# Half-swapped V by DMA instead of GpSimd, first loads dealt anew over three queues, a warm-up on a constant and new scheduler durations, in a fused attention and gated-MLP kernel

## The chip, the cores and the metric

One core of one Trainium2 chip. The metric is the device time of one launch in microseconds (us); the median of several executions is quoted, with the lowest and the highest.

## The reference, cut to what matters

```python
# x: 1 x 2048 x 512, bf16; 32 heads of 16; 4 segments of 512 rows; F = 1792
q, k, v = x @ wq, x @ wk, x @ wv              # split into heads and segments
for s in range(4):                            # segments, in order
    p = softmax(qs @ ks.T * scale + causal_mask)
    a_dot = p @ vs                            # "PV"
    a_mem = (phi(qs) @ M) / (phi(qs) @ z + 1e-6)
    o = sigmoid(beta) * a_mem + (1 - sigmoid(beta)) * a_dot
    M, z = M + phi(ks).T @ vs, z + phi(ks).sum()   # the memory ("mz")
a = concat(o) @ wo
b = (relu(x @ W_gate) * (x @ W_up)) @ W_down
g = sigmoid((x * gate_w).sum(-1))             # one gate per row
out = g * a + (1 - g) * b
```

The memory carries from segment to segment; everything else is free to be interleaved.

## The kernel before: the parts that matter

The program is a list of operations with dependencies, assumed durations and buffers. A small scheduler orders them at build time, engine by engine. So a changed duration, dependency or buffer count changes the whole order on every engine.

PV contracts over 64 keys at a time in a 64 x 32 tiling. For half of the blocks the V rows stand in the wrong half of the partitions, so a second copy of V with the halves swapped (VS) is kept. Before, GpSimd made it, two copies for each of 16 blocks of 128 rows:

```python
    def proj_v(s, t):                       # V of segment s, rows 128*t..
        ...
        if t == 0:
            VS[s] = Buf(VSp)                # VSp: 2 buffers, only the heads needed
        for r in range(2):
            def f(e, r=r):
                src = Vp[s].t[64 - 64 * r:128 - 64 * r, t, 0:H * HP]...   # the other half
                nc.gpsimd.tensor_copy(VS[s].t[64 * r:64 * r + 64, t, ...], src[:, :, r, 0:DH])
```

The start: x in four parts on the SyncE and ScalarE queues, wq in three parts on GpSimd's, 28 warm-up matmuls on a tile that VectorE first sets, and wk held back by a dependency until a copy of x is done:

```python
    for i in range(2):
        for eng, q, h in (("SP", nc.sync, 0), ("ACT", nc.scalar, 1)):
            ...                              # x part (i, h)
    for n, (c0, c1) in enumerate(((0, 1), (1, 2), (2, 4))):
        ...  nc.gpsimd.dma_start(out=wq_sb[:, c0:c1, :], ...)
    o_wk0 = op("wk0", {"DVE": 0.08}, ..., key=-490)        # opens wk's load

    def c_dummy(e):
        for _ in range(28):
            nc.tensor.matmul(g_dummy.t[:, 0:P], lhsT=zero[:, 0:P], rhs=zero[:, 0:P], ...)
```

Three transfers on SyncE's queue: the transposes of phi(k) (tile pK) that feed the memory update, the load of the next segment's x (tile xn) that feeds the row gate g, and the weights of the MLP.

```python
                nc.sync.dma_start_transpose(out=pK[s].t[:, :, c * P:(c + 1) * P], in_=src.t[:])
    ...
            nc.sync.dma_start(out=xn[s].t[:], in_=x[s * L:(s + 1) * L, :]...)
```

The softmax here doesn't subtract the row's maximum and nothing guards it: scores larger than these inputs give would overflow.

Of the kernel before, what the change touches and what calls it, by code (L numbers as in the profile page):

```python
# [26 lines left out]
VSW = H // 2 * HP + 16  # L27

MM = 0.216
SW = 0.1  # L30
# [136 lines left out]
def kernel(  # L167
# [52 lines left out]
    VSp = pool("VS", 2, [P, 4, VSW])  # L220
# [5 lines left out]
    zero = osp.tiles[0]  # L226
# [25 lines left out]
    def c_zero(e):  # L252
        nc.vector.memset(zero[:, 0:P], 1.0)  # L253
    o_zero = op("zero", {"DVE": 0.15}, c_zero, cls=0, key=-100)
# [7 lines left out]
    def c_warm(e):  # L262
        nc.scalar.activation(scratch[:], zero[:, 0:1], ACT.Exp)
# [10 lines left out]
    def c_vones(e):  # L274
        for t in Vpp.tiles + VSp.tiles:
            nc.gpsimd.memset(t[:].rearrange("p a b -> p (a b)"), 1.0)
    o_vones = op("vones", {"POOL": 6.2}, c_vones, key=-60)
# [11 lines left out]
    def c_dummy(e):  # L289
        for _ in range(28):  # L290
            nc.tensor.matmul(g_dummy.t[:, 0:P], lhsT=zero[:, 0:P], rhs=zero[:, 0:P], start=True, stop=True)  # L291
# [21 lines left out]
    for i in range(2):  # L313
        for eng, q, h in (("SP", nc.sync, 0), ("ACT", nc.scalar, 1)):
            def f(e, i=i, q=q, h=h):
                q.dma_start(out=xn[0].t[:, 2 * h:2 * h + 2, 256 * i:256 * i + 256],
                            in_=x[256 * h:256 * h + 256, 256 * i:256 * i + 256].rearrange("(t p) d -> p t d", p=P))
            lx0[i, h] = load(f"x0_{i}{h}", f, 131072, -300 + i, eng=eng, alloc=[xn[0]] if (i, h) == (0, 0) else [],
                             uses=[] if (i, h) == (0, 0) else [xn[0]])
    for n, (c0, c1) in enumerate(((0, 1), (1, 2), (2, 4))):  # L320
        def f(e, c0=c0, c1=c1):
            nc.gpsimd.dma_start(out=wq_sb[:, c0:c1, :], in_=A_wq[c0 * P:c1 * P, :].rearrange("(c p) n -> p c n", p=P))
        o = op(f"wq{c0}", {"POOL": 1.0}, f, key=-110 + 15 * n, cls=0, land=131072 * (c1 - c0) / GBs)
        for ci in range(c0, c1):
            lwq[ci] = [o]
    o_vones.deps.append((lwq[3][0], -1e9))
# [8 lines left out]
    o_wk0 = op("wk0", {"DVE": 0.08}, lambda e: nc.vector.memset(wk_sb[0:1, 0, 0:1], 0.0), key=-490, cls=0)  # L335
# [67 lines left out]
    for ci in range(NC):  # L403
        def f(e, ci=ci):
            for c in range(NC):
                nc.tensor.matmul(qS.t[:, c, :], lhsT=wq_sb[:, ci, c * P:(c + 1) * P], rhs=xT[0].t[:, ci, :],  # L406
                                 start=(ci == 0), stop=(ci == NC - 1))
        o_q0 = op(f"q0.{ci}", {"PE": 4 * MM * (1.5 if ci < 2 else 1)}, f,
                  deps=xc0[ci] + lwq[ci] + [(o_q0, 0.0) if ci else None],
                  key=-400 + ci, mode="D", alloc=[qS] + q0 if ci == 0 else [], uses=([] if ci == 0 else [qS]) + [xT[0]])  # L410
        if ci < 2:
            first_x(ci + 2, o_q0)
# [165 lines left out]
    def proj_v(s, t):  # L578
# [12 lines left out]
        if t == 0:  # L591
            VS[s] = Buf(VSp)
        o_vs[s, t] = []
        for r in range(2):
            def f(e, r=r):
                src = Vp[s].t[64 - 64 * r:128 - 64 * r, t, 0:H * HP].rearrange("p (h r v) -> p h r v", r=2, v=HP)
                nc.gpsimd.tensor_copy(  # L597
                    VS[s].t[64 * r:64 * r + 64, t, 0:H // 2 * HP].rearrange("p (h v) -> p h v", v=HP)[:, :, 0:DH],
                    src[:, :, r, 0:DH])
            o_vs[s, t].append(op(f"vs{s}{t}{r}", {"POOL": 0.5}, f, deps=[o_v[s, t]] + (o_vs[s, t - 1] if t else []),  # L600
                                 key=a.key + 4, cls=2, alloc=[VS[s]] if t == 0 and r == 0 else [],
                                 uses=[Vp[s]] + ([] if t == 0 and r == 0 else [VS[s]])))
# [13 lines left out]
    def mz_deps(s):  # L616
        return [o_pKt[s, c] for c in range(NC)] + [o_v[s, t] for t in range(4)]
# [21 lines left out]
    def mz0():  # L639
        g = Buf(G)  # L640
        k = dkey(3)
        a = op("mz0", {"PE": 0.5}, lambda e: mz_mm(0, g), deps=mz_deps(0), key=k, mode="C", alloc=[g], uses=[pK[0], Vp[0]])
        mz_after(0, a, g, k)
# [76 lines left out]
    def unit(i):  # L720
# [8 lines left out]
        for n, parts in enumerate(FL):  # L729
# [12 lines left out]
            a = op(f"f{s}{c}.{n}", {"PE": MM}, f,  # L742
# [36 lines left out]
    def dens(s, k0, org):  # L779
# [12 lines left out]
        if mds:  # L792
            gm = Buf(G)
            rec_of[s, "mz"] = am = op(f"mz{s}", {"PE": 0.5}, lambda e: mz_mm(s, gm), deps=[(a, 0.0)], key=k0 - 20, mode="C",
                                      alloc=[gm], uses=[pK[s], Vp[s]])
            gate_mz.append((s, am, gm, k0))
# [34 lines left out]
    def rest(i, E, masks, behind):  # L831
# [4 lines left out]
        def f(e):  # L836
            for kb in range(8):
                src, off = E[kb]
                w = L - 64 * kb
                for r in range(2):  # L840
                    rows = slice(64 * r, 64 * r + 64)
                    for j in range(4):
                        if kb % 2 == r:
                            h = 8 * c + 2 * j + r
                            v = Vp[s].t[rows, kb // 2, h * HP:h * HP + 32]
                        else:
                            h = 4 * c + j
# [3 lines left out]
        a = op(f"pv{s}{c}", {"PE": 1.05}, f,  # L851
               deps=[(m, MG) for m in masks] + [o_v[s, t] for t in range(4)] + [o for t in range(4) for o in o_vs[s, t]] +
# [172 lines left out]
```

## Time and profile before

| | before |
|---|---|
| time, median of six (lowest to highest) | 266.87 us (266.46 to 267.45) |
| span of the profiled execution | 265.3 us |
| TensorE busy | 257.0 us |
| ScalarE, GpSimd, VectorE busy | 193.9, 191.0, 183.8 us |
| warm-up ends and x is transposed | 4.08 us |
| q's first step, k's first matmul | 5.19, 9.60 us |

The prediction below shows the lines of the page, the waits and the start. These are two lines of the timeline of the kernel before, first SyncE's queue, then VectorE. The columns of the timeline are start and duration in us, engine (SPq is SyncE's queue), line, operation, output and input, count, and in brackets the idle time before it and what ended it.

```profile
22.71 0.37 SPq L359 DMA_DIRECT2D xn<-in_A_x_dram  x1
...
28.27 0.75 DVE L461 SCALAR_TENSOR_TENSOR xn<-xn,gwrep 128x512 bf16<-128x512 bf16 x1
```

Segment 1's x is issued at 22.71 and VectorE begins the row gate on it at 28.27, with no bracket: it did not wait. The load landed at 26.16, so it had 2.1 us to spare.

### The profile page before, as it was taken

Reading aid. Unit: us, or ns where it says so; the run is one execution under the profiler, and the core shown is the slowest. Engines: PE = TensorE matmul, PEld = TensorE weight load, DVE = VectorE, ACT = ScalarE, POOL = GpSimd, SP = SyncE. Lnnn points to the kernel's source line nnn. Section 1 sums busy time; section 2 is a strip of 40 time slices with the busy share of each in tenths; the row PEclk is TensorE's granted clock in tenths of the full one; section 3 lists DMA queues with packets and bytes.
Section 4 is the critical chain, followed back from the end, with each engine's and each line's share of the span. In section 5 each row is a group of like instructions: output and inputs, shape, how many; then the busy total and the mean of one; then the engine's idle time right before and its main releaser. Section 6 shows DMA issues by size and latency. Waiting matters only on the chain.

```text
span 265.3 us, 7048 instructions
## 1 busy us (share of the span) xinstructions
PE 257.0 (97%) x2808; PEld 115.9 (44%) x2844; DVE 183.8 (69%) x407; ACT 193.9 (73%) x189; POOL 191.0 (72%) x470
## 2 busy tenths in 40 slices
PE   8999999999999999999999999999999999999995
PEld 6433444444454444444434434344443444344444
DVE  1497888888975285998888837688985735566611
ACT  3598999899885558999896668898788566777010
POOL 8678888888559788798648988887878866537000
PEclk9999999999999999999999999999999999999999
DMA  5997990017310100000551010000000010000011
GB/s 162 289 252 203 313 261 13 4 40 80 100 26 1 42 20 22 0 2 2 132 88 23 21 42 20 4 2 0 2 0 4 0 42 23 20 2 0 2 41 40
DMA packets 27057, 15.54 MB, mean 59 GB/s; under 512 B 13584, under 2 KB 26896, under 8 KB 27024
## 3 DMA queue, kind: packets, MB, share of 16 engines
q1 hardware_dynamic: 26304, 14.30, 22.0%
q0 software_dynamic: 176, 0.52, 0.6%
q8 instruction: 22, 0.36, 0.6%
q10 hardware_dynamic: 544, 0.26, 0.3%
q14 instruction: 11, 0.09, 0.1%
HBM read 9.84 MB, written 2.10 MB: 45 GB/s over the span
## 4 chain that ended last, share of the span: by engine, by line
PE 97%; issue 2%; DVE 0%; ACT 0%; DVEq 0%
PE G L248 74%; PE S L738 9%; PE G L849 7%; PE G L246 3%; PE S L406 2%; PE G L291 1%; PE G L611 1%; PE G L785 0%; PE G L385 0%; DVE os L700 0%; ACT xT L395 0%; DVE os L253 0%; DVE mcole L268 0%; DVEq L700 0%; DVE mcol L267 0%
## 5 line engine op out<-in xcount | busy, mean ns | idle before, releaser
L752 ACT ACTIVATE E<-S 128x2048 bf16<-128x2048 f32 x72 | 135.1, 1876 | 34.3 <-PE S L738 31.9
L760 POOL TENSOR_SCALAR_AFFINE_SELECT E<-E 64x256 bf16<-64x256 bf16 x256 | 115.7, 452 | 38.5 <-ACT E L752 24.6
L248 PE MATMUL G<-xT,wu_sb 128*128 128x512 bf16 x211 | 57.3, 380 | 0.4 <-issue 0.2
L248 PE MATMUL G<-xT,wg_sb 128*128 128x512 bf16 x206 | 56.2, 380 | 1.1 <-issue 0.8
L663 DVE TENSOR_TENSOR hT<-G,os 128x512 bf16<-128x512 f32 x56 | 38.2, 684 | 19.7 <-ACT os L659 10.7
L248 PE MATMUL G<-wd_sb,hT 128*128 128x512 bf16 (+1 forms) x212 | 48.9, 365 | 1.1 <-issue 1.0
L884 DVE STREAM_TRANSPOSE T<-G 128x512 f32<-128x512 f32 x44 | 30.3, 702 | 14.0 <-PE G L849 8.2
L659 ACT ACTIVATE os<-G 128x512 bf16<-128x512 f32 x56 | 32.7, 597 | 6.1 <-PE G L248 5.3
L248 PEld LDWEIGHTS <-wu_sb 128*128 128x128 bf16 x218 | 19.9, 98 | 24.8 <-issue 3.0
L248 PEld LDWEIGHTS <-wg_sb 128*128 128x128 bf16 x218 | 19.4, 98 | 24.6 <-issue 4.1
L248 PEld LDWEIGHTS <-hT 128*128 128x128 bf16 x222 | 20.3, 98 | 22.3 <-issue 2.6
L738 PE MATMUL S<-QT,K 32*128 32x192 bf16 (+7 forms) x512 | 28.6, 287 | 0.5
L738 PEld LDWEIGHTS <-K 32*128 32x128 bf16 x512 | 8.2, 92 | 30.4 <-issue 29.9
L700 DVE TENSOR_SCALAR os<-G,ngcol 128x512 bf16<-128x512 f32 (+1 forms) x10 | 7.0, 697 | 19.4 <-PE G L248 19.3
L849 PE MATMUL G<-E,Vp 64*32 64x128 bf16 (+7 forms) x512 | 19.0, 284 | 0.2 <-issue 0.2
L849 PE MATMUL G<-E,VS 64*32 64x128 bf16 (+7 forms) x512 | 18.4, 284 | 0.0
L248 PE MATMUL G<-wo_sb,oT 128*128 128x512 bf16 (+1 forms) x66 | 17.2, 367 | 0.3 <-issue 0.3
L597 POOL COPY VS<-Vp 64x256 bf16<-64x256 bf16 x32 | 13.3, 416 | 4.8 <-DVE Vp L515 3.3
L904 DVE TENSOR_TENSOR O<-T,sm 128x256 bf16<-128x256 f32 x32 | 15.8, 524 | 0.3
L248 PE MATMUL G<-xT,wk_sb 128*128 128x512 bf16 x60 | 15.8, 380 | 0.3 <-issue 0.2
L702 ACT ACTIVATE os<-G,ngcol 128x512 bf16<-128x512 f32 x7 | 4.8, 687 | 15.0 <-PE G L248 15.0
L479 POOL COPY R<-rcol 32x4 f32<-32x4 f32 x64 | 13.5, 210 | 3.0
(98 smaller groups left out, 302.0 us busy)
## 6 DMA issues: line engine op xcount, KB each, us to landing
out_dram<-os SPq DMA_DIRECT2D x15, 128.0 KB, 1.7
wd_sb<-in_B_W_down_dram SPq DMA_DIRECT2D x1, 1792.0 KB, 13.4
xn<-in_A_x_dram SPq DMA_DIRECT2D x3, 512.0 KB, 4.7
wg_sb<-in_B_W_gate_dram SPq DMA_DIRECT2D x2, 512.0 KB, 5.8
wu_sb<-in_B_W_up_dram SPq DMA_DIRECT2D x2, 512.0 KB, 6.9
wg_sb<-in_B_W_gate_dram SPq DMA_DIRECT2D x3, 256.0 KB, 6.9
wu_sb<-in_B_W_up_dram SPq DMA_DIRECT2D x3, 256.0 KB, 7.2
wk_sb<-in_A_wk_dram SPq DMA_DIRECT2D x1, 512.0 KB, 4.0
```

Of the source, the lines that this page charges most:

```text
L246: nc.tensor.matmul(out_ap[q], lhsT=lhsT[:, q], rhs=rhs, start=start, stop=stop, tile_position=(0, 32 * j))
L248: nc.tensor.matmul(out_ap, lhsT=lhsT, rhs=rhs, start=start, stop=stop)
L479: nc.gpsimd.tensor_copy(R[s][32 * j:32 * j + 32, k, :], rcol[32 * k:32 * k + 32, cols])
L597: nc.gpsimd.tensor_copy(VS[s].t[64 * r:64 * r + 64, t, 0:H // 2 * HP].rearrange("p (h v) -> p h v", v=HP)[:, :, 0:DH], src[:, :, r, 0:DH])
L659: nc.scalar.activation(rg.t[:], g.t[:], ACT.Relu)
L663: nc.vector.tensor_tensor(h.t[:], u.t[:], rg.t[:], ALU.mult)
L738: nc.tensor.matmul(sp.t[:, j, off:off + w], lhsT=K2[s, cc].t[rows, kb, :, :].rearrange("p r k -> p (r k)"), rhs=QT[s, cc].t[rows, L - w:L] ...
L752: nc.scalar.activation(eb_.t[:], sp.t[:], ACT.Exp, scale=SCALE)
L760: nc.gpsimd.affine_select(out=v, in_=v, compare_op=ALU.is_ge, fill=0.0, base=0, pattern=[[0, 4], [1, 64]], channel_multiplier=-1)
L849: nc.tensor.matmul(gs[r].t[32 * j:32 * j + 32, L - w:L], lhsT=v, rhs=src.t[rows, j, off:off + w], start=(kb == 0), stop=(kb == 7), tile_po ...
L884: nc.vector.transpose(T.t[:].rearrange("p b e -> p (b e)"), g.t[:])
L904: nc.vector.tensor_tensor(O.t[:, :, r, :], T.t[:, :, 0:DH], sm.t[:, r, :, None].to_broadcast([P, 16, DH]), ALU.mult)
```

## The change

Its intent: take the 32 V copies off GpSimd (13.3 us), deal the parts of x and wq anew over the three queues, start the warm-up without waiting for VectorE, and tell the scheduler durations closer to those measured. The core of the diff:

```diff
-MM = 0.216
-SW = 0.1
+MM = 0.2159
+SW = 0.094
...
-    VSp = pool("VS", 2, [P, 4, VSW])
+    VSp = pool("VS", 1, [P, 4, VW])
...
-        nc.vector.memset(zero[:, 0:P], 1.0)
+    ones = nc.const_aps.tensor(1.0, [P, P], BF16)
...
-        for _ in range(28):
-            nc.tensor.matmul(g_dummy.t[:, 0:P], lhsT=zero[:, 0:P], rhs=zero[:, 0:P], ...)
+        for _ in range(31):
+            nc.tensor.matmul(g_dummy.t[:, 0:P], lhsT=ones, rhs=ones, ...)
...
+    x0_part(0, 0, "SP", -300)
+    x0_part(0, 1, "ACT", -300)
+    wq_part(0, 1, "ACT", -299)
+    x0_part(1, 0, "SP", -299)
+    x0_part(1, 1, "POOL", -110)
+    wq_part(1, 2, "POOL", -95)
+    wq_part(2, 4, "POOL", -80)
...
-    o_wk0 = op("wk0", ..., key=-490, cls=0)
+    o_wk0 = op("wk0", ..., key=-600, cls=0)
...
+            if ci == 0:                      # two fillers before q's first step
+                for _ in range(2):
+                    nc.tensor.matmul(qS.t[:, 0, 0:P], lhsT=ones, rhs=ones, ...)
...
-                nc.gpsimd.tensor_copy(VS[s].t[64 * r:64 * r + 64, t, ...], src[:, :, r, 0:DH])
+            def f(e):                        # once per segment, after its last V block
+                for r in range(2):
+                    a, b = slice(64 * r, 64 * r + 64), slice(64 - 64 * r, 128 - 64 * r)
+                    nc.sync.dma_start(out=VS[s].t[a], in_=Vp[s].t[b])
...
-        a = op(f"pv{s}{c}", {"PE": 1.05}, f,
+        a = op(f"pv{s}{c}", {"PE": 1.015}, f,     # three more durations likewise
```

More of the change, by code (lines that the diff above doesn't have):

```diff
@@ L26 @@
 VW = H * HP + 16
-VSW = H // 2 * HP + 16
-MM = 0.216
-SW = 0.1
+MM = 0.2159
+SW = 0.094
 MG = 1.0
@@ L225 @@
     osp = rgp = pool("os", 4, [P, D])
-    zero = osp.tiles[0]
     smp = pool("sm", 3, [P, 2, 16], F32)
@@ L249 @@
     ACTC = lambda n: 0.19 + 0.000833 * n
-    def c_zero(e):
-        nc.vector.memset(zero[:, 0:P], 1.0)
-    o_zero = op("zero", {"DVE": 0.15}, c_zero, cls=0, key=-100)
+    ones = nc.const_aps.tensor(1.0, [P, P], BF16)
+    o_zero = op("zero", {"DVE": 0.15}, lambda e: None, cls=0, key=-100)
     def c_ident(e):
@@ L262, in c_warm @@
     def c_warm(e):
-        nc.scalar.activation(scratch[:], zero[:, 0:1], ACT.Exp)
+        nc.scalar.activation(scratch[:], ones[:, 0:1], ACT.Exp)
     o_warm = op("warm", {"ACT": 1.5}, c_warm, deps=[o_zero], cls=0, key=-100)
@@ L274, in c_vones @@
     def c_vones(e):
-        for t in Vpp.tiles + VSp.tiles:
+        for t in Vpp.tiles:
             nc.gpsimd.memset(t[:].rearrange("p a b -> p (a b)"), 1.0)
-    o_vones = op("vones", {"POOL": 6.2}, c_vones, key=-60)
+    o_vones = op("vones", {"POOL": 4.2}, c_vones, key=-60)
     def c_bdm(e):
@@ L289, in c_dummy @@
     def c_dummy(e):
-        for _ in range(28):
-            nc.tensor.matmul(g_dummy.t[:, 0:P], lhsT=zero[:, 0:P], rhs=zero[:, 0:P], start=True, stop=True)
+        for _ in range(31):
+            nc.tensor.matmul(g_dummy.t[:, 0:P], lhsT=ones, rhs=ones, start=True, stop=True)
     g_dummy = Buf(G)
@@ L312, with first_load, x0_part, wq_part @@
     lx0, lw, lwq = {}, {}, {}
-    for i in range(2):
-        for eng, q, h in (("SP", nc.sync, 0), ("ACT", nc.scalar, 1)):
-            def f(e, i=i, q=q, h=h):
-                q.dma_start(out=xn[0].t[:, 2 * h:2 * h + 2, 256 * i:256 * i + 256],
-                            in_=x[256 * h:256 * h + 256, 256 * i:256 * i + 256].rearrange("(t p) d -> p t d", p=P))
-            lx0[i, h] = load(f"x0_{i}{h}", f, 131072, -300 + i, eng=eng, alloc=[xn[0]] if (i, h) == (0, 0) else [],
-                             uses=[] if (i, h) == (0, 0) else [xn[0]])
-    for n, (c0, c1) in enumerate(((0, 1), (1, 2), (2, 4))):
-        def f(e, c0=c0, c1=c1):
-            nc.gpsimd.dma_start(out=wq_sb[:, c0:c1, :], in_=A_wq[c0 * P:c1 * P, :].rearrange("(c p) n -> p c n", p=P))
-        o = op(f"wq{c0}", {"POOL": 1.0}, f, key=-110 + 15 * n, cls=0, land=131072 * (c1 - c0) / GBs)
+    QUEUE = {"SP": nc.sync, "ACT": nc.scalar, "POOL": nc.gpsimd}
+    def first_load(name, eng, key, nbytes, out_ap, in_ap, alloc=(), uses=()):
+        o = load(name, lambda e: QUEUE[eng].dma_start(out=out_ap(), in_=in_ap), nbytes, key, eng=eng, alloc=alloc, uses=uses)
+        if eng == "POOL":
+            o.engs["POOL"] = 0.9
+        return o
+    def x0_part(i, h, eng, key):
+        first = not lx0
+        lx0[i, h] = first_load(f"x0_{i}{h}", eng, key, 131072,
+                               lambda: xn[0].t[:, 2 * h:2 * h + 2, 256 * i:256 * i + 256],
+                               x[256 * h:256 * h + 256, 256 * i:256 * i + 256].rearrange("(t p) d -> p t d", p=P),
+                               alloc=[xn[0]] if first else [], uses=[] if first else [xn[0]])
+    def wq_part(c0, c1, eng, key):
+        o = first_load(f"wq{c0}", eng, key, 131072 * (c1 - c0), lambda: wq_sb[:, c0:c1, :],
+                       A_wq[c0 * P:c1 * P, :].rearrange("(c p) n -> p c n", p=P))
         for ci in range(c0, c1):
             lwq[ci] = [o]
+    x0_part(0, 0, "SP", -300)
[5 more added lines that the diff above has]
+    wq_part(2, 4, "POOL", -80)
     o_vones.deps.append((lwq[3][0], -1e9))
@@ L334 @@
     lw["wk"] = loadw("wk", wk_sb, A_wk, 0, D, 1)
-    o_wk0 = op("wk0", {"DVE": 0.08}, lambda e: nc.vector.memset(wk_sb[0:1, 0, 0:1], 0.0), key=-490, cls=0)
+    o_wk0 = op("wk0", {"DVE": 0.08}, lambda e: nc.vector.memset(wk_sb[0:1, 0, 0:1], 0.0), key=-600, cls=0)
     lw["wk"].deps.append((o_wk0, None))
@@ L404, in f @@
         def f(e, ci=ci):
+            if ci == 0:
+                for _ in range(2):
+                    nc.tensor.matmul(qS.t[:, 0, 0:P], lhsT=ones, rhs=ones, start=True, stop=True)
             for c in range(NC):
@@ L590, in proj_v @@
                        uses=[g, Vp[s]])
-        if t == 0:
+        if t == 3:
             VS[s] = Buf(VSp)
-        o_vs[s, t] = []
-        for r in range(2):
-            def f(e, r=r):
-                src = Vp[s].t[64 - 64 * r:128 - 64 * r, t, 0:H * HP].rearrange("p (h r v) -> p h r v", r=2, v=HP)
-                nc.gpsimd.tensor_copy(
-                    VS[s].t[64 * r:64 * r + 64, t, 0:H // 2 * HP].rearrange("p (h v) -> p h v", v=HP)[:, :, 0:DH],
-                    src[:, :, r, 0:DH])
-            o_vs[s, t].append(op(f"vs{s}{t}{r}", {"POOL": 0.5}, f, deps=[o_v[s, t]] + (o_vs[s, t - 1] if t else []),
-                                 key=a.key + 4, cls=2, alloc=[VS[s]] if t == 0 and r == 0 else [],
-                                 uses=[Vp[s]] + ([] if t == 0 and r == 0 else [VS[s]])))
+            def f(e):
+                for r in range(2):
+                    a, b = slice(64 * r, 64 * r + 64), slice(64 - 64 * r, 128 - 64 * r)
+                    nc.sync.dma_start(out=VS[s].t[a], in_=Vp[s].t[b])
+            o_vs[s] = op(f"vs{s}", {"SP": 1.2}, f, deps=[o_v[s, t] for t in range(4)], key=a.key + 4, cls=0, land=2.5,
+                         alloc=[VS[s]], uses=[Vp[s]])
     W2 = 2 * (DH + 1)
@@ L641, in mz0 @@
         k = dkey(3)
-        a = op("mz0", {"PE": 0.5}, lambda e: mz_mm(0, g), deps=mz_deps(0), key=k, mode="C", alloc=[g], uses=[pK[0], Vp[0]])
+        a = op("mz0", {"PE": 0.56}, lambda e: mz_mm(0, g), deps=mz_deps(0), key=k, mode="C", alloc=[g], uses=[pK[0], Vp[0]])
         mz_after(0, a, g, k)
@@ L741, in f @@
                                          tile_position=(32 * j, 0))
-            a = op(f"f{s}{c}.{n}", {"PE": MM}, f,
+            a = op(f"f{s}{c}.{n}", {"PE": 0.229}, f,
                    deps=[o_q[s, cc] for cc in chunks] + [o for cc in chunks for o in o_k2[s, cc]] +
@@ L793, in dens @@
             gm = Buf(G)
-            rec_of[s, "mz"] = am = op(f"mz{s}", {"PE": 0.5}, lambda e: mz_mm(s, gm), deps=[(a, 0.0)], key=k0 - 20, mode="C",
+            rec_of[s, "mz"] = am = op(f"mz{s}", {"PE": 0.56}, lambda e: mz_mm(s, gm), deps=[(a, 0.0)], key=k0 - 20, mode="C",
                                       alloc=[gm], uses=[pK[s], Vp[s]])
@@ L842, in f @@
                     for j in range(4):
+                        h = 8 * c + 2 * j + r
                         if kb % 2 == r:
-                            h = 8 * c + 2 * j + r
                             v = Vp[s].t[rows, kb // 2, h * HP:h * HP + 32]
                         else:
-                            h = 4 * c + j
                             v = VS[s].t[rows, kb // 2, h * HP:h * HP + 32]
@@ L850, in f @@
                                          start=(kb == 0), stop=(kb == 7), tile_position=(64 * r, 32 * j))
-        a = op(f"pv{s}{c}", {"PE": 1.05}, f,
-               deps=[(m, MG) for m in masks] + [o_v[s, t] for t in range(4)] + [o for t in range(4) for o in o_vs[s, t]] +
+        a = op(f"pv{s}{c}", {"PE": 1.015}, f,
+               deps=[(m, MG) for m in masks] + [o_v[s, t] for t in range(4)] + [o_vs[s]] +
                ([(behind, 0.0)] if behind else []),
```

## The prediction

> **What bounds the kernel now.** I read the head of the page first, for the engines' shares; then the chain of work that ended last; then the waits, for TensorE's own; then the timeline of the first ten microseconds, because half of the change lies there.
>
> ```profile
> span 265.3 us, 7048 instructions
> PE 257.0 (97%) x2808; PEld 115.9 (44%) x2844; DVE 183.8 (69%) x407; ACT 193.9 (73%) x189; POOL 191.0 (72%) x470
> ...
> PE 97%; issue 2%; DVE 0%; ACT 0%; DVEq 0%
> ```
>
> TensorE (PE) is busy for 257.0 of 265.3 us, and the chain, followed back from the last instruction, lies on it for 97%. GpSimd (POOL), from which the change takes work, is not in the chain at all.
>
> ```profile
> ACT E L752 <- PE S L738: 31.9, 43, 2.4
> ...
> POOL E L760 <- ACT E L752: 24.6, 26, 2.1
> ...
> PE G L248 <- issue: 2.4, 15, 0.2
> ...
> PE G L291 <- DVE mcole L268: 1.1, 1, 1.1
> ...
> L597 POOL COPY VS<-Vp 64x256 bf16<-64x256 bf16 x32 | 13.3, 416 | 4.8 <-DVE Vp L515 3.3
> ```
>
> The first four lines are from the waits (who waited for whom: total us, times, longest), the last from the page's groups. ScalarE waits for TensorE and GpSimd waits for ScalarE; TensorE's own waits are the 1.1 us before its first warm-up matmul and crumbs of at most 0.2 us, some of which are missing matmul records. The 32 half-swapped copies of V cost GpSimd 13.3 us, all beside TensorE.
>
> ```profile
> 0.89 0.17 DVE L253 MEMSET os<- 128x128 bf16 x1 [0.89 <-PEq L1009]
> ...
> 1.12 3.17 PE L291 MATMUL G<-os 128*128 128x128 bf16 x28 [1.12 <-DVE mcole L268]
> ...
> 4.08 1.06 PE L385 MATMUL G<-ident,xn 128*128 128x128 bf16 x8
> ...
> 5.18 1.54 PE L406 MATMUL S<-xT,wq_sb 128*128 128x512 bf16 x4
> ...
> 5.31 0.37 SPq L331 DMA_DIRECT2D wk_sb<-in_A_wk_dram  x1
> ...
> 6.79 1.03 PE L406 MATMUL S<-xT,wq_sb 128*128 128x512 bf16 x4
> ...
> 9.60 2.75 PE L248 MATMUL G<-xT,wk_sb 128*128 128x512 bf16 x12
> ```
>
> The warm-up (28 matmuls) ends where the transposes of x start, at 4.08: the first loads are already there. Their queue rows say so: issue at 0.8 plus the 2.8 to 3.1 us to landing that the page lists gives 3.6 to 3.9. Then q's four projection steps and k follow with one gap of 0.25 us (4.94 to 5.19, the copy of x to SBUF). From 5.2 us to the end I find no true idle on TensorE.
>
> [...]the 28 warm-ups take 3.17 us with the last one's tail, 107 ns apart[...], q's first step takes 1.54 us and the second 1.03 us. The full clock came at about 6.3 us here[...].
>
> [...]
>
> ```profile
> 19.18 0.59 PE L248 MATMUL G<-xT,wg_sb 128*128 128x512 bf16 x2
> 19.70 0.40 PE L738 MATMUL S<-QT,K 32*128 32x384 bf16 x8
> 20.03 0.61 PE L248 MATMUL G<-xT,wg_sb 128*128 128x512 bf16 x2
> ```
>
> Dense matmuls stand 0.216 us apart, so two of them from 19.18 end at 19.61; the row-tiled scores start at 19.70.
>
> [...]
>
> **The change part by part.**
>
> 1. V's half-swap. Removed: 32 GpSimd copies, 13.3 us, and two memsets of 1.13 us, 2.2 us. GpSimd falls from 191.0 to about 175.5 us; on the path: 0. Added: four pairs of copies of 64 x 2368 bf16 (303 KB each).[...] The buffer is now single, so segment 1's pair waits for segment 0's last PV block. Counting the built program's TensorE instructions at the trace's durations, that block ends near 75 us and the next PV block starts 17 us later; the later segments have some 16 and 14 us, and the first pair can be issued near 21 us and is needed near 33. [...]0 on the path.
>
> 2. The order on TensorE. The scheduler, given new durations, orders differently. Counting both built programs: tiling changes go from 170 to 174, 4 x 0.094 = +0.38 us; matmuls split over column tiles go from 37 to 11. Split matmuls cost the same or slightly more (in the chain, 48 quarters, that is 12 matmuls, take 2.59 to 2.73 us; 12 plain ones 2.70), so 26 fewer give 0 to -0.2 us. All other matmuls are the same. Sum: +0.2 us.
>
> 3. Warm-up. The constant is ready before the opening barrier, so TensorE starts at about 0.83 instead of 1.12: -0.29 us. But 31 warm-ups instead of 28 add 3 x 0.107 = +0.32, and the transposes still follow: +0.03 us. Two more before q's first step fill most of the 0.25 us gap in which TensorE waits for the copy of x anyway: 0 to +0.02 us.[...]
>
> 4. First loads. wq's first part goes to ScalarE's queue and the last x part to GpSimd's. q's first step waits for the copy of x, not for wq; wq was issued at 1.31 and took 3.2 to 3.6 us, thus landed by 4.9, in time for 5.19. So 0 us. wk's gate opens after the first copy (4.83) rather than after the second (5.20): wk issues 0.3 us sooner. It landed at 5.31 + 4.0 = 9.31 and was first used at 9.60: 0 us, except that in an execution with an early clock the old kernel would have waited for it and the new one would not (at most -0.2 us).
>
> Sum: +0.2 + 0.05 - 0.15 - 0.05 = +0.05 us, plus what the next rival may cost.
>
> **The rivals.**
>
> A: a DMA takes the place of GpSimd as a wait. The tightest point is segment 1's memory update. SyncE issues in order; the pair for segment 1 (waiting for the PV block) stands ahead of the last transpose of pK, and the denominator matmul after it waits for that transpose. In the new order 23 dense matmuls and two score fills lie between: 23 x 0.216 + 2 x 0.23 + 4 x 0.094 = 5.8 us. The two issues (about 0.5 us each, like the loads' queue rows) and the transpose's 2.5 us to landing make 3.5 us[...].[...] Against: the issue times overlap the transfer. Worth 0 to +1 us here; I give it one chance in three, +0.2 us on average. In the crowded start the weights behind the first pair slip by some 2 us: the tightest (the up weights first used near 36 us, landed near 31) keeps 3 us.
>
> B: lighter GpSimd makes the masks earlier, PV and the score pipeline move up, and TensorE saves stalls. Against: TensorE has no stalls to save after 5.2 us. At most -0.3 us.
>
> C: the startup is really bound by loads, and three queues bring x forward by a microsecond. Against: the transposes start exactly at the warm-up's end, and now there are more warm-ups. It could only help if the clock turned full before 4 us. At most -0.8 us.
>
> D: one more engine is tipped over: ScalarE takes some five more evacuations from VectorE (0.6 us each, 3 us of 194 busy). It was waiting for TensorE for 32 us, so no.
>
> **Range and chances.** 266.96 + 0.05 + 0.2 is about 267.2; B and C pull the mean a little the other way, so I set 267.0. The three runs before spread over 0.7 us[...]; with A at one end (+1) and B and C at the other, 266.1 to 268.2 should hold it eight times in ten. 2% is 5.3 us: no part is near it. Faster by 2%: 0.02; within: 0.95; slower: 0.03, for a DMA wait in several segments at once.
>
> **What would show it.** Right: TensorE again 97%, busy 257 us within 0.5; POOL near 175 us; no TensorE wait on DMA over 0.3 us; the transposes of x again near 4.1 us; q's first step near 5.2 us[...]. Wrong: a TensorE row naming VS or pK among the waits (A), a first k matmul clearly before 9.2 us without an early clock (C), or TensorE's busy time falling by more than 1 us, which would mean that the split matmuls or the tiling changes cost something other than I read.

The sum was +0.05 us, one of its terms -0.15 us for an earlier full clock (part 3), and without it the sum is +0.2 us. What a change of the tiling costs is what the fence shows: 19.61 to 19.70, 0.09 us.

## The result and the profile after

| | before | changed |
|---|---|---|
| median of six (lowest to highest) | 266.87 us (266.46 to 267.45) | 267.31 us (266.92 to 267.98) |
| ratio | | 1.0017, 95% interval 0.9999 to 1.0035 |

The ratio is the mean time of one kernel's fast runs over that of the other's of the same rounds, so it is not quite the ratio of the medians.

The profiled execution of the changed kernel happened to be the slowest of its six (267.98). So it was profiled once more later (run after_again, 266.64 us). The first fence is from the page of the first profile, the second from that of the second.

```profile
span 266.3 us, 6941 instructions
PE 260.7 (98%) x2771; PEld 114.6 (43%) x2771; DVE 177.3 (67%) x400; ACT 197.8 (74%) x195; POOL 175.2 (66%) x436
PE 92%; DMA 3%; DVE 2%; issue 1%; POOL 1%; POOLq 0%; DVEq 0%
VS<-Vp SPq DMA_DIRECT2D x8, 296.0 KB, 4.2
```

```profile
PE 257.4 (97%) x2735; PEld 115.1 (43%) x2771; DVE 177.5 (67%) x400; ACT 197.7 (75%) x195; POOL 175.8 (66%) x436
PE 97%; issue 1%; DVE 1%; DVEq 0%
```

GpSimd fell by 15.8 us (191.0 to 175.2) and VectorE by 6.5, ScalarE rose by 3.9, and the time did not move. The eight copies land 4.2 us after their issue in the median. In the first profile DMA has entered the chain with 3%; in the second it is not there. The busy time of 260.7 us in the first should not be compared with the 257.0 of before: there all 2771 matmul records are present, while the kernel before lacks 36 (2808 of 2844 weight loads) and the second profile also lacks 36 (2735 of 2771). Records that are missing leave holes. 257.4 against 257.0 is the fair pair.

What put DMA into the first chain stands in its waits (engine, line, waited for; total us, times, longest):

```profile
POOL E L772 <- ACT E L764: 43.1, 34, 6.1
...
DVE xn L476 <- DMA xn<-in_A_x_dram: 1.4, 1, 1.4
```

GpSimd now waits for ScalarE for 43.1 us instead of 24.6: the freed time turned into idling. And VectorE waits 1.4 us for the x load that had 2.1 us to spare before. The timeline of the changed kernel's first profile shows the rest (SyncE's queue, VectorE, TensorE):

```profile
20.90 1.17 SPq L612 DMA_DIRECT2D VS<-Vp  x2
22.16 2.50 SPq L589 DMA_TRANSPOSE pK<-pk  x1
24.84 0.46 SPq L371 DMA_DIRECT2D xn<-in_A_x_dram  x1
...
29.24 0.89 DVE L476 SCALAR_TENSOR_TENSOR xn<-xn,gwrep 128x512 bf16<-128x512 bf16 x1 [1.38 <-DMA xn<-in_A_x_dram]
...
33.89 1.02 PE L246 MATMUL G<-xT,wu_sb 128*128 128x512 bf16 x4 [0.65 <-DVE hT L675]
```

The first VS pair and a transpose held in its place stand ahead of the x load, which is issued 2.1 us later than before (24.84 against 22.71). The products hT stand behind the gate in VectorE's order and come late with it, and TensorE waits 0.65 us. That is one of two extra losses in this execution. The other is a pause near 46 us in the second PV block: 0.73 us between two of its matmuls that usually follow at once, with no semaphore that explains it (more on it under no_split). From k's first matmul to the last matmul start this execution took 253.76 us, the second profile 252.38; the 1.38 us between them are 0.72 (the start-to-start excess at 33.9) + 0.56 (the pause, 0.73 against 0.17) + 0.10.

The start, in the same first profile:

```profile
0.83 3.24 PE L288 MATMUL G<-const-bfloat16-1.0 128*128 128x128 bf16 x31 [0.83 <-PEq L1020]
3.91 0.61 PE L397 MATMUL G<-ident,xn 128*128 128x128 bf16 x8
...
4.76 1.02 PE L421 MATMUL S<-xT,wq_sb 128*128 128x512 bf16 x4
...
7.36 1.90 PE L421 MATMUL S<-xT,wq_sb 128*128 128x512 bf16 x8 [0.27 <-DMA wq_sb<-in_A_wq_dram]
```

TensorE starts at 0.83 instead of 1.12. The eight transposes take 0.61 us instead of 1.06, so the full clock was there before 4 us (the trace's clock record has it from 3.67 us on, that of the kernel before from 6.27); q's first step starts at 4.76 instead of 5.19. Then 0.43 us of that is given back, start to start, to wq's last part. k starts at 9.10.

### The profile page after: what moved, and what is told of

The parts are those of the page before. It is cut to its first block, busy times and chain, and to the rows that moved or that the text cites. A ratio compares the mean times of both kernels' runs of the same rounds, so it can differ in the third digit from the quotient of the medians.

```text
span 266.3 us, 6941 instructions
## 1 busy us (share of the span) xinstructions
PE 260.7 (98%) x2771; PEld 114.6 (43%) x2771; DVE 177.3 (67%) x400; ACT 197.8 (74%) x195; POOL 175.2 (66%) x436
## 4 chain that ended last, share of the span: by engine, by line
PE 92%; DMA 3%; DVE 2%; issue 1%; POOL 1%; POOLq 0%; DVEq 0%
PE G L246 75%; PE S L750 8%; PE G L860 6%; DMA xn<-in_A_x_dram 2%; DMA wq_sb<-in_A_wq_dram 1%; DVE xn L476 1%; PE S L421 1%; PE G L244 1%; PE G L623 1%; DVE hT L675 0%; PE G L797 0%; POOL xn L313 0%; POOL wq_sb L313 0%; DVE os L712 0%; DVE pk L560 0%
## 5 line engine op out<-in xcount | busy, mean ns | idle before, releaser
L772 POOL TENSOR_SCALAR_AFFINE_SELECT E<-E 64x256 bf16<-64x256 bf16 x256 | 116.4, 455 | 56.8 <-ACT E L764 43.1
L246 PE MATMUL G<-xT,wu_sb 128*128 128x512 bf16 x224 | 59.6, 380 | 0.6 <-DVE hT L675 0.6
L246 PE MATMUL G<-xT,wg_sb 128*128 128x512 bf16 x224 | 59.5, 380 | 0.0
L246 PE MATMUL G<-wd_sb,hT 128*128 128x512 bf16 (+1 forms) x238 | 54.5, 367 | 0.0
L246 PEld LDWEIGHTS <-hT 128*128 128x128 bf16 x238 | 21.7, 98 | 24.1 <-issue 3.0
L246 PEld LDWEIGHTS <-wg_sb 128*128 128x128 bf16 x224 | 20.2, 98 | 25.6 <-issue 4.3
L714 ACT ACTIVATE os<-G,ngcol 128x512 bf16<-128x512 f32 x9 | 6.2, 687 | 16.6 <-PE G L246 15.8
L712 DVE TENSOR_SCALAR os<-G,ngcol 128x512 bf16<-128x512 f32 (+1 forms) x8 | 5.4, 679 | 17.6 <-PE G L246 17.6
L860 PEld LDWEIGHTS <-Vp 64*32 64x32 bf16 x512 | 12.2, 91 | 7.7 <-issue 3.2
L937 POOL TENSOR_TENSOR O<-O,O 128x512 bf16<-128x512 bf16 x11 | 13.1, 1186 | 3.6 <-DVE O L915 2.9
L246 PE MATMUL G<-wv_sb,xT 128*128 128x512 bf16 x64 | 15.3, 380 | 0.0
```

The source lines that it names most:

```text
L246: nc.tensor.matmul(out_ap, lhsT=lhsT, rhs=rhs, start=start, stop=stop)
L712: nc.vector.tensor_scalar(ob.t[:, cs], g.t[:, 0:W], ngcol[:, tt:tt + 1], None, ALU.mult)
L714: nc.scalar.activation(ob.t[:, cs], g.t[:, 0:W], ACT.Copy, scale=ngcol[:, tt:tt + 1])
L772: nc.gpsimd.affine_select(out=v, in_=v, compare_op=ALU.is_ge, fill=0.0, base=0, pattern=[[0, 4], [1, 64]], channel_multiplier=-1)
L860: nc.tensor.matmul(gs[r].t[32 * j:32 * j + 32, L - w:L], lhsT=v, rhs=src.t[rows, j, off:off + w], start=(kb == 0), stop=(kb == 7), tile_po ...
L937: (nc.vector if e == "DVE" else nc.gpsimd).tensor_tensor(Oa.t[:], Oa.t[:], Ob.t[:], ALU.add)
```

## The experiments

Theory 1: every part of the change lies beside TensorE's work; what differs is an order worth 0.2 us and loads that are at the edge of need. Rivals: the V copies cost about half a microsecond that the start gives back (two effects that cancel); or rival A of the prediction (the memory update of segment 1 waits); or a real gain at the start that is lost in a new load wait.

Times of three batches, five rounds each except after_again. The first (start_only, v_gpsimd, no_split, xn_first) and the third (v_only, dur_only, v_extra1) have eleven runs of the kernel before each; the twelve of the second are those of the first and one more. "k to last" is the time from k's first matmul to the last matmul start in the profiled execution, which leaves the start out.

| run | what it is | median us (range) | ratio to before, 95% | q, k start | k to last |
|---|---|---|---|---|---|
| (before, profile) | | 266.92, 266.93, 266.56 in the three batches | | 5.19, 9.60 | 252.26 |
| (changed, profile) | | 267.31 (266.92 to 267.98) | 1.0017 [0.9999, 1.0035] | 4.76, 9.10 | 253.76 |
| start_only | before + new start | 267.24 (266.39 to 267.39) | 1.0010 [0.9997, 1.0023] | 5.20, 9.22 | 252.04 |
| v_only | before + V by DMA | 267.24 (266.48 to 267.48) | 1.0014 [0.9999, 1.0030] | 5.19, 9.96 | 252.17 |
| dur_only | before + durations | 266.95 (266.76 to 268.54) | 1.0018 [0.9998, 1.0038] | 5.20, 9.68 | 252.13 |
| v_gpsimd | changed, V by GpSimd | 267.08 (266.75 to 267.68) | 1.0008 [0.9996, 1.0020] | 5.20, 9.58 | 252.32 |
| no_split | changed, no split matmuls | 266.97 (266.79 to 267.39) | 1.0004 [0.9992, 1.0016] | 4.71, 9.31 | 252.42 |
| xn_first | changed, x load before VS | 267.24 (266.84 to 267.30) | 1.0007 [0.9995, 1.0019] | 5.19, 9.70 | 252.48 |
| after_again | changed | 266.64 (one) | | 5.20, 9.15 | 252.38 |
| no_warm | changed, 1 warm-up | 267.39 (267.38 to 268.08) | 1.0017 [1.0003, 1.0032] | 4.67, 10.71 | 252.25 |
| best_start | new start, wq re-queued | 267.56 (266.21 to 267.96) | 1.0016 [0.9999, 1.0034] | 4.56, 9.28 | 251.88 |
| v_extra1 | changed, 1 extra copy | 267.82 (267.07 to 268.60) | 1.0047 [1.0027, 1.0066] | 5.20, 9.39 | 253.33 |
| v_twice | changed, copies doubled | 282.50 (280.40 to 284.75) | 1.0575 [1.0540, 1.0609] | 5.20, 9.44 | 267.64 |

All outputs are right.

### The three parts, each alone on the kernel before

**start_only** takes the loads, the warm-up, the fillers and wk's gate, and leaves V, the durations and the order on every engine from q on as they were.

```diff
+    x0_part(0, 0, "SP", -300)  ...  wq_part(2, 4, "POOL", -80)
-        for _ in range(28):   (on zero)
+        for _ in range(31):   (on the constant), and two fillers before q
```

> The kernel before with the startup part alone (loads on three queues, earlier gate for wk, warm-up on the constant); every engine's order after the startup is that of before. My theory (the startup is worth little on average[...]): 0 to -0.4 us against before. Rival (the startup is the change's whole gain and the rest loses it again): -0.8 us or more. In the profile: first k matmul between 9.0 and 9.6 us; the last q parts wait for wq (0.3 to 0.5 us) if the full clock comes before 5 us.

267.24 us, ratio 1.0010: no gain. In the profile k started 0.38 us earlier than in that of before (9.22 against 9.60); k's first weight load still waited 0.21 us for wk there. That execution took 266.39 us, 0.58 less than the profiled one of before (266.97), but it is the shortest of its five; nothing of this can be seen in the median.

**v_only** takes the VS copies by DMA and the durations that belong to them; the scheduler then gives another order.

```diff
-                nc.gpsimd.tensor_copy(VS[s]..., src)          # 8 per segment
+                    nc.sync.dma_start(out=VS[s].t[a], in_=Vp[s].t[b])   # 2 per segment
```

> The kernel before with the DMA half-swap alone: old startup, old assumed durations except those of the removed copies; the scheduler gives it an order of its own (169 tiling changes and 33 split matmuls against 170 and 37 before, so by my count of TensorE work 0.12 us less than before). Theory 'V's copies were beside TensorE's work and their removal is worth nothing': 266.5 to 267.3, ratio 0.9985 to 1.0015, GpSimd about 175 us. Rival 'moving V costs about 0.5 us and the start gives it back': 267.3 to 267.8, with a TensorE wait that names pK, VS or x.

267.24 us, ratio 1.0014, k to last 252.17 (before 252.26). It fits the first theory. The rival wanted a TensorE wait that names pK, VS or x; the profile has none. But its median is near the rival's lower edge too, so the time alone would not decide; the profile does.

**dur_only** takes the six numbers of the scheduler's model alone.

```diff
-MM = 0.216; SW = 0.1; "pv": 1.05; "mz": 0.5 (twice); "f": MM
+MM = 0.2159; SW = 0.094; "pv": 1.015; "mz": 0.56 (twice); "f": 0.229
```

> The kernel before with only the six changed numbers of the scheduler's model of TensorE; same copies, same start. The order on TensorE changes at many places; 171 tiling changes and 15 split matmuls against 170 and 37, by my count 0.06 us less TensorE work than before. Theory 'the order is worth at most a few tenths': 266.6 to 267.4. If split matmuls cost more than plain ones by 0.05 us or more each (the other reading that I left open), 22 fewer would give 1 us: 265.9 or less.

266.95 us and k to last 252.13. 22 split matmuls fewer changed nothing that can be seen. So a split matmul (four quarters over column tiles) costs what a plain one does, within some 0.03 us (an estimate: the interval of 0.5 us over 22; the order changed with it).

The three parts do not show two effects that cancel. Each alone is within 0.2% of before, like the whole.

### Parts taken out of the changed kernel

**v_gpsimd** puts the eight GpSimd copies per segment back, into two compact buffers, at the place of the pair in the list; the order of the other engines stays that of the changed kernel.

```diff
-                    nc.sync.dma_start(out=VS[s].t[a], in_=Vp[s].t[b])
+                for t in range(4):
+                    for r in range(2):
+                        nc.gpsimd.tensor_copy(VSx[s % 2][64 * r:64 * r + 64, t, ...], src)
```

> The changed kernel with the V copies made by GpSimd again, eight in a row per segment, into two compact buffers; the order of TensorE, VectorE and ScalarE is that of the changed kernel, SyncE's lacks the pairs. Theory 1: the wait near 33.9 us is gone (x load 2 to 3 us sooner), time 0.5 to 0.7 us below the changed kernel. Rival (the new order, not the DMA, costs the time): TensorE still waits there, time as the changed kernel or up to 1 us more, because GpSimd delays the masks. GpSimd busy near 190 us.

267.08 us, ratio 1.0008. Segment 1's x landed at 26.35 (26.16 before; 29.21 changed) and VectorE began the gate at 28.24 without a wait. That shows that the pair is what pushes the x load. The time shows that the push costs nothing that five rounds resolve.

**xn_first** moves the first pair behind the x load on SyncE's queue; nothing else.

```diff
+    moved = next(o for o in order if o.name == "vs0")
+    order.remove(moved)
+    order.insert(next(i for i, o in enumerate(order) if o.name == "xn1") + 1, moved)
```

> The changed kernel, with one difference: on SyncE's queue the first pair of V copies is issued after the last-but-one pK transpose and the second x load instead of before them; all other engines' orders are unchanged. Theory 1 (the pair holds back the x load, VectorE stands in order behind it, and TensorE then waits 0.65 us for a PSUM buffer near 33.9 us): x lands 2 to 3 us sooner, VectorE's wait of 1.4 us for it and TensorE's 0.65 us are gone, and the time falls by 0.5 to 0.7 us against the changed kernel, to about that of before or less. Rival (the order of VectorE's work alone makes the wait): TensorE still waits 0.5 us or more there, time unchanged within 0.2 us.

x landed at 27.53, VectorE began at 28.36 without a wait, TensorE did not wait near 33 us, and the time was 267.24. So the wait of the first profile can be removed, and removing it does not make the kernel faster. But the move is not free: segment 0's memory update now waits 0.28 us, start to start, for its last transpose of pK, which landed at 43.12. The first line is TensorE, the second its weight loads:

```profile
42.51 0.92 PE L623 MATMUL G<-Vp,pK 128*32 128x34 bf16 x64
...
43.16 0.17 PEld L623 LDWEIGHTS <-pK 128*32 128x32 bf16 x16 [0.21 <-DMA pK<-pk]
```

Reading the same place in the other traces shows the tightest point of the changed kernel. This transpose landed 2.1 us before its 16 matmuls started in the kernel before and 2.4 us in v_gpsimd, but only 0.1 us in after_again and 0.5 us in the changed kernel's first profile, no_split and v_extra1.

**no_split** emits the matmuls that the scheduler had split as plain ones (8 matmuls; two more tiling changes).

```diff
-            tiling[0] = o.ran
+            tiling[0] = o.mode
```

> The changed kernel with the eight column-split dense matmuls issued as plain ones (24 instruction pairs fewer, two tiling changes more: +0.19 us by the prediction's count). Theory 3 (the pause of 0.73 us inside segment 0's second PV block at 46 us[...]): the pause moves or shrinks to below 0.4 us, time -0.2 to -0.6 us against the changed kernel. Rival (the pause is a wait on data): it stays at 0.7 us in the same block, time +0.2 us.

266.97 us, k to last 252.42. It has the changed kernel's order on SyncE, and its x load landed at 28.41; VectorE waited 0.38 us, TensorE did not. In this run too q started early, at 4.71 (4.76 in the changed kernel's first profile), and 0.69 us were then lost, start to start, to wq's last part: k at 9.31.

The run was made for the pause near 46 us, and that is gone from the PV block, as theory 3 expected. The kept traces say more. Six profiles have the pause (before, changed, after_again, v_only, dur_only, v_extra1: 0.15 to 0.73 us). In each of them it ends 2.3 to 2.4 us after a transfer of 16 KB begins on the DMA queue that the page calls "instruction" (in the first profile at 44.26, for a pause that ends at 46.67). In the three of the changed order it stands at the same instruction. No run moved that transfer alone, so whether the pause comes from it is not shown.

**after_again** is the changed kernel, unaltered.

> The changed kernel once more, unaltered, for a second profile. If the wait of TensorE at 33.9 us (0.65 us for hT, behind the x load) belongs to this program, it is there again with the x load at 29 us; if it belonged to one execution whose loads were slow, the x load lands at 27.5 to 28.7 and TensorE does not wait there. The pause near 46 us (0.76 us, no semaphore) should change its size and place in the same way. Which of the two clock phases it shows (transposes full speed at 3.9 or only at 6.3) is open.

From its timeline, VectorE and TensorE at the place of the wait:

```profile
28.39 0.77 DVE L476 SCALAR_TENSOR_TENSOR xn<-xn,gwrep 128x512 bf16<-128x512 bf16 x1 [0.54 <-DMA xn<-in_A_x_dram]
...
33.16 1.04 PE L246 MATMUL G<-xT,wu_sb 128*128 128x512 bf16 x3
```

VectorE waits 0.54 us for x, and TensorE's matmul has no bracket: no wait. The pause near 46 us (here at 45.2) is 0.17 us. So both losses of the first profile belonged to that execution, not to the program. What does belong to the program is that VectorE waits for x at 28.4. Some 0.7 us of such waiting is free (1.38 us of it cost TensorE 0.65), so it is close to the edge.

### What the start could give

**no_warm** has one warm-up matmul and no fillers.

```diff
-        for _ in range(31):
+        for _ in range(1):
-                for _ in range(2):   (the fillers)
+                for _ in range(0):
```

> The changed kernel with one warm-up matmul instead of 31 and without the two fillers before q; the orders are else identical. It shows what the warm-up is worth and hence how much an earlier start of it could ever give. [...]the transposes start when x lands (3.5 to 3.9 us) at the half clock, the full clock comes[...] (near 7 to 9 us), q's four steps then cost 0.5 us each more; k starts at 10 to 11 us instead of 9.1 to 9.7, and the time is 0.8 to 2.0 us longer than the changed kernel's. Rival (the start is bound by the loads of wq and wk and not by the clock, so the warm-up is idle filling): k starts within 0.3 us of 9.3 and the time is the same within 0.3 us.

In the profile it went as the first theory said: x was transposed at 3.46, as soon as it landed, the half clock lasted to 8.91 (two steps of four q matmuls took 1.89 and 1.91 us before that, the eight from there 1.97), and k started at 10.71. That execution took 268.08 us. But the other three took 267.38 to 267.39, and the ratio, 1.0017, is that of the changed kernel. So the expected loss of 0.8 to 2.0 us was not confirmed: over executions it is 0 with an uncertainty of some 0.6 us (the two intervals). Why the profile's later k does not show in the other executions stays open; when the full clock came in them was not recorded.

**best_start** is start_only with wq's last part (two of its four quarters) on SyncE's queue behind the second x load, and 28 warm-ups.

```diff
-    wq_part(2, 4, "POOL", -80)
+    wq_part(2, 4, "SP", -298)
-        for _ in range(31):
+        for _ in range(28):
```

> The kernel before with the new startup (V still copied by GpSimd, the old order), wq's last two parts moved from GpSimd's queue to SyncE's, right behind the second x load, and 28 warm-up matmuls instead of 31. It takes away the wait that the profile of the changed kernel showed for wq's last part (0.43 us; 0.69 us in the run without split matmuls). If the start was held by that load: no wait for wq, transposes at 3.8 to 4.0, k at 8.7 to 9.3 us, and the time is 0.3 to 0.6 us below the startup part alone (267.24), about 266.7. Rival ([...]wk's landing near 9.0 then holds k anyway): k stays at 9.0 to 9.7 and the time stays within 0.2 us of 267.1.

It failed: 267.56 us in the median. The profiled execution took 266.21 us, the shortest of all, so its trace cannot say what held the other five; that stays open. It shows one limit. The wait for the last part is gone, and now the part before it is late:

```profile
6.46 0.82 PE L422 MATMUL S<-xT,wq_sb 128*128 128x512 bf16 x3 [0.63 <-DMA wq_sb<-in_A_wq_dram]
```

With an early clock (eight transposes in 0.61 us, from 3.71) q started at 4.56, and k still only at 9.28. The load moved forward moved another back: the part before it took 3.6 us from issue to landing, against 2.7 in the changed kernel. wk had landed at 8.70 here, so it was not what held k. In the three profiles with the full warm-up and an early start of q (this one, changed, no_split: 4.56, 4.76, 4.71) k started at 9.1 to 9.3 us, each time after a wait for a part of wq.

### Rival A, with the dose raised

The prediction named segment 1's memory update as the tightest point: SyncE issues the pair ahead of the last transpose of pK. This is that place in after_again (SyncE's queue, then TensorE):

```profile
74.58 1.11 SPq L612 DMA_DIRECT2D VS<-Vp  x2
75.80 2.51 SPq L589 DMA_TRANSPOSE pK<-pk  x1
...
80.20 0.40 PE L797 MATMUL G<-pq,Z 128*32 128x512 bf16 x4
80.43 0.72 PE L623 MATMUL G<-Vp,pK 128*32 128x34 bf16 x64
```

The transpose took 4.2 us to land, thus at 80.0: 5.4 us after the pair's issue. The last 16 of the 64 matmuls read it. The 64 starts spread over 0.55 us, so three quarters of that put the last 16 at 80.84, or 6.25 us after the pair's issue. The margin is 0.8 us. The transpose lands later behind a pair: there it took 4.2 us to land, without a pair ahead of it (v_gpsimd) 3.0, and in no_split, where it was issued 1 us later behind the pair, 3.4; it landed 0.5 us after the pair's second copy both times.

**v_twice** issues each pair twice, over the same rows, so that the second pair also waits for the first to land.

```diff
-                for r in range(2):
+                for r in (0, 1, 0, 1):
```

> The changed kernel with each of the four pairs of half-swap copies issued twice (the same data; 16 copies instead of 8; nothing else altered). It doubles the suspected cost. Theory 1 (the pair stands ahead of segment 1's x load on SyncE's queue and pushes it to the edge of need, so that only the first pair matters and only beyond the slack): x lands 2 to 4 us later than in the changed kernel, near 32, VectorE waits 3 us or more for it, TensorE then waits near 33 to 36 us for hT by some 2 to 4 us, and the time is 269 to 271 us, ratio to before 1.008 to 1.016. Rival A as I predicted it (segment 1's memory update behind the pK transpose): the loss appears near 90 us instead, named by pK or the denominator. Rival 'the copies are hidden with room to spare': under 0.3 us more, ratio up to 1.002.

282.5 us: 15 us lost, far beyond the theory's 2 to 4 us and in more places. The timeline at the same place (segment 1):

```profile
79.59 5.14 SPq L612 DMA_DIRECT2D VS<-Vp  x4
...
84.83 1.55 SPq L589 DMA_TRANSPOSE pK<-pk  x1
...
89.91 0.28 PE L623 MATMUL G<-Vp,pK 128*32 128x34 bf16 x16 [3.90 <-DMA pK<-pk]
...
91.11 3.04 PE L246 MATMUL G<-wd_sb,hT 128*128 128x512 bf16 x7 [0.16 <-issue]
...
95.60 2.76 PE L246 MATMUL G<-wd_sb,hT 128*128 128x512 bf16 x12
```

Exactly the 16 matmuls of the last transpose wait, 3.90 us. Segment 2's update waits 2.97 us in the same way, and segment 1's x load costs TensorE 2.13 + 0.73 us near 34 to 36 us (VectorE waited 4.3 us for it). Together 9.7 us. The last two lines show where the rest went: after the wait 7 matmuls take 3.04 us (0.43 us each), a little later 12 take 2.76 (0.22 each). TensorE had fallen back to half its clock. The stretches of the same trace give its cost (from left: stretch, length, busy time of TensorE, weight loads, VectorE, ScalarE and GpSimd with counts, granted clock, DMA share, GB/s):

```profile
92.00:94.00 2.00, 2.00 (x7) 0.65 (x5) 0.00 (x0) 1.20 (x1) 1.92 (x7) 0.50 0.19 66
94.00:96.00 2.00, 2.00 (x11) 0.67 (x10) 0.00 (x0) 0.56 (x1) 1.44 (x4) 0.83 0.00 0
```

With 0.81 in the stretch before these, the clock withheld (0.19 + 0.50 + 0.17) x 2 us = 1.7 us of work. The other two places (near 36 and 160 us) cost 1.7 us each in the same way, so 5.1 us in all. The three stretches at half clock, from 36.65, 91.26 and 159.53, lasted 3.41 us each. 9.7 + 5.1 = 14.8 us, of 15.6 between the two spans (280.5 and 264.9).

So both places are real, theory 1's and rival A's. Each is just short of costing anything in the changed kernel; segment 0's memory update (see xn_first) is a third.

**v_extra1** adds a single copy, in segment 1 only. It is issued behind the pair over the rows of the first copy, and so waits for that one to land.

```diff
-                for r in range(2):
+                for r in ((0, 1, 0) if s == 1 else (0, 1)):
```

> The changed kernel with one extra copy in segment 1 only: the first half of the pair is issued again behind the pair (the same data over the same rows, so it first waits for the first copy to land); everything else is as in the changed kernel. A half dose at the place that rival A named. In the profiles of the changed kernel the last transpose of pK lands about 5.4 us after the pair's first issue and is needed after 5.6 to 5.7 us, a margin of 0.2 to 0.4 us without any wait; with both copies doubled everywhere TensorE waited 3.9 us there. Theory 'margin of about 0.3 us, then every microsecond counts': the transpose is issued 2 to 3.5 us later, TensorE waits 1.5 to 3 us for pK near 83 us, nowhere else on a DMA, and the time is 268.5 to 271 us (ratio 1.006 to 1.014, more if the clock falls to half after the wait). Rival 'the loss with doubled copies came from the start and from the clock, not from this place': under 0.5 us more than the changed kernel's 267.3.

```profile
74.88 3.74 SPq L612 DMA_DIRECT2D VS<-Vp  x3
78.71 1.53 SPq L589 DMA_TRANSPOSE pK<-pk  x1
...
80.72 0.58 PE L623 MATMUL G<-Vp,pK 128*32 128x34 bf16 x48
82.09 0.28 PE L623 MATMUL G<-Vp,pK 128*32 128x34 bf16 x16 [0.79 <-DMA pK<-pk]
```

The place and the name are as expected, no other TensorE wait names a DMA, and 267.82 us is slower than before (ratio 1.0047, the only interval beside v_twice's that lies well above 1). That is 0.3% or 0.8 us more than the changed kernel's 1.0017, the size of the wait, though the two intervals leave some 0.7 us either way; k to last is 0.95 us longer than in after_again. The size was missed: 0.8 us of wait instead of 1.5 to 3. I had taken the margin from the denominator's matmuls (80.20); the 16 that wait come later. With the margin read from those 16, the three runs agree:

| run | pair issued to transpose landed | pair issued to the 16 due | difference | idle before the 16 |
|---|---|---|---|---|
| after_again | 5.4 us | 6.25 us | -0.8 | none |
| v_extra1 | 7.2 us | 6.25 us | 0.9 | 0.79 |
| v_twice | 10.3 us | 6.25 us | 4.0 | 3.90 |

The landing is the issue of the transpose plus its time to landing (for v_twice 84.83 + 5.0). At this place, in these three runs, up to 0.8 us of lateness was free, and from there every microsecond was paid. The clock stayed full after v_extra1's short wait: 1.00 granted from 82 to 84 us and from 84 to 86.

## Why the prediction was right

**What bounds the kernel: right.** TensorE is still 97% of the chain and busy for 257.4 us (predicted: 257 within 0.5). Nothing that left the other engines could show. One sentence was wrong: "From 5.2 us to the end I find no true idle on TensorE". The kernel before has a pause of 0.34 us near 45.7 us, and the executions of the changed one have 0.17 and 0.73 there; v_only, dur_only and v_extra1 have 0.15 to 0.28. No semaphore explains it; the transfer told under no_split begins before it each time, but its cause is not shown.

**Part 1, V's swap: right on GpSimd, incomplete on the queue.** GpSimd went to 175.2 us (predicted 175.5). The pair in segment 1 was complete 4.9 to 5.0 us after its issue (in after_again the second copy, at 75.11, took 4.4 us to land); in segments 0 and 3 it took 4.7 to 4.9. In segment 2, where transposes and other loads share the queue, it took 6.7 and 7.5 us in the two profiles, which the forecast did not foresee; the first use came 8 us later still. The step that failed is the last of rival A: "the tightest (the up weights ...) keeps 3 us". I checked the weights behind the first pair and not the x load beside them, nor the transposes of segment 0's memory update, which also come later (margin 0.1 to 0.5 us instead of 2.1). The x load had 2.1 us to spare and slipped by 2.2 to 3.0 us in landing, so VectorE waited 0.3 to 1.4 us for it in the four profiles of this order at full warm-up (v_extra1, no_split, after_again, changed). In one execution TensorE felt it; in the median it costs nothing that was resolved.

**Part 2, the order: right within the scatter.** k to last is 251.88, 252.04 and 252.26 in the order of before (best_start, start_only, before), and 252.25 to 252.48 in five undisturbed profiles of the changed order (no_warm, v_gpsimd, after_again, no_split, xn_first). The means are 0.3 us apart, predicted 0.2, but the two ranges touch. That split matmuls are free was left as "0 to -0.2"; dur_only and no_split found nothing.

**Part 3, the warm-up: right that it is worth little.** The transposes started at 3.91 and 4.09 (predicted near 4.1). The 0.15 us that an earlier start was to save, the term cut above, was the author's estimate and was not shown: even taking the warm-up away did not move the median. The full clock did not come at one time: the last matmul at half clock came at 3.6 us in one execution of the changed kernel and at 4.9 in the other, and in the profile of the kernel before the clock record turns full at 6.27. What sets it no run shows.

**Part 4, the loads: the sum right, one term wrong.** Of an execution with an early clock the prediction said that the old kernel would wait for wk "and the new one would not". The old start did wait in dur_only (TensorE 0.23 us for wk, k at 9.68). The new one waits as well: for wq's last part (0.43 and 0.69 us) or for wk (k's first weight load waited 0.38 us in after_again). The gain that rival C allowed, up to 0.8 us, did begin in the first profile (q 0.43 us earlier), and the same 0.43 us went into wq.

**Rival A: the place and the mechanism right, and it did not happen.** (Segment 0's update, not named, is tighter still.) The transpose landed 5.4 us after the pair's issue. The prediction's 5.8 us of work between left out the four quarters of the denominator and the first 48 matmuls of the update, 0.2 + 0.4 us; with them it is 6.4, measured 6.25. So there is a margin of 0.8 us where the prediction had about none, and the +0.2 us that I gave it were 0 in these profiles.

**B and D: as argued.** GpSimd's freed time became waiting for ScalarE (24.6 to 43.1 us). ScalarE gained 3.9 us of work (predicted 3) without effect.

**The range.** 266.1 to 268.2 is five times as wide as the 0.44 us between the two medians. That the result lies in it says little; what speaks for the mechanism is the parts taken one by one.

No variant beat the kernel before. All but the two with extra copies lie within 0.2% of it.

## What to carry to other kernels

Here one engine carries 97% of the chain, and taking 16 us of work off another was worth nothing that the times resolve (v_only: GpSimd from 191.0 to 174.8 us, ratio 1.0014); read instead what the moved work now stands in front of. The pair of copies added on SyncE's queue cost not its own 4.7 to 4.9 us to landing but the slack of what stands behind it (the x load had 2.1 us to spare, and then VectorE waited 0.3 to 1.4 us for it): for each of those transfers take issue to landing and compare it with when the exact instruction that reads it is due. And a wait that was long enough cost twice on TensorE. In v_twice a wait of 3.90 us, one of 2.97 us, and one of 2.13 us with a second of 0.73 us behind it were each followed by the half clock, at 1.7 us of lost work apiece; after 0.79 us in v_extra1 the clock stayed full.
